# Token mixing and attention in one TensorE queue: the second half of the token mixing counted at twice its cost

## The chip, the cores and the metric

The kernel runs on one core of one Trainium2 chip. The metric is the time of one execution on the device, in microseconds (us), the median of several runs. Everything is float32.

A core has five engines that run beside each other, each with its own queue of instructions, worked off in the order in which the program issued them: TensorE (PE, matrix products, with a separate row PEld for loading weights), VectorE (DVE), ScalarE (ACT), GpSimd (POOL), and SyncE (SP), which here only starts DMA transfers. TensorE writes its products into PSUM, from where VectorE or ScalarE has to take them before the same buffer can be written again.

## The reference

Attention with normalised queries and keys for 8 batches, 12 heads, 448 positions and 64 columns, followed by an MLP mixer on the result:

```python
q_n, k_n = rmsnorm(q, g_q), rmsnorm(k, g_k)
scores = q_n @ k_n^T / sqrt(64)
attn = exp(scores - max);  attn = attn / (sum(attn) + 1e-9)
x = (attn @ v), heads side by side          # (8, 448, 768)

h  = relu(x^T @ w_tok1) @ w_tok2            # token mixing, inner size 256
u  = x + h^T
h2 = relu(u @ w_ch1) @ w_ch2                # channel mixing, inner size 1536
out = u + h2
```

## The kernel before

The kernel works batch by batch and always one batch ahead with the attention: while the mixer of batch b runs, the attention of batch b+1 is computed. The two are independent, and all of it goes through the same five queues. The program decides the order: it makes lists of work items, each a pair of an estimated cost (about microseconds) and a function that issues its instructions, and merges the lists:

```python
def merge(*lists):
    totals = [sum(c for c, _ in l) or 1.0 for l in lists]
    done = [0.0] * len(lists)
    at = [0] * len(lists)
    res = []
    while True:
        live = [i for i in range(len(lists)) if at[i] < len(lists[i])]
        if not live:
            return res
        i = min(live, key=lambda i: (done[i] + lists[i][at[i]][0] / 2) / totals[i])
        c, fn = lists[i][at[i]]
        at[i] += 1
        done[i] += c
        res.append((c, fn))
```

So the lists advance at the same share of their own totals. A cost has no other use but one: run() adds the costs up as a clock, by which a few DMA transfers are issued some microseconds later than the work that prepares them:

```python
def run(items):
    for c, fn in items:
        fn()
        clock[0] += c
        while pending and pending[0][0] <= clock[0]:
            pending.pop(0)[1]()
```

The main loop, with cuts:

```python
for b in range(B):
    early, double = middle_items(b)      # tok2, moving sums, ch1 | ch2, two columns of weights
    if b == 0:
        ...                              # batch 0 has a path of its own
    else:
        if in_next(b - 1):
            y, z = sends(b - 1, [0, 1, KC, KC + 1]), left
            left = [y[0], y[1], z[0], y[2], z[1], y[3]]
        run(merge(tok1_items(b, 0), left[:2]))
        begin, early = merge(tok1_items(b, 1) + early[:3 * KC], left[2:]), early[3 * KC:]
        if b == 1:
            early, double = merge(begin + early, sums[12:33]), merge(double, sums[33:])
            begin = []
        early = begin + early + double
    lo = (b + AHEAD) * per + 1
    att = []
    if b + AHEAD < B:
        att = att_items(lo, lo + 10) + x_items(b + AHEAD, 0) + att_items(lo + 10, lo + per)
    tail = 4
    early, last = early[:-tail], early[-tail:]
    if b + 1 < B:
        last = merge(last, x_items(b + 1, 1))
    run(merge(att, early) + last + last_items(b, sums[6:12]))
    left = turns(b, [2, KC + 2])
```

The items of the mixer, with their costs (us(n, cols) is n * cols * 4 / 2400):

- tok1, cost 2.56: four products of 384 columns (L638), then a ReLU on ScalarE. The first half of the token mixing is tok1 of the first 384 channels, and nothing of the attention lies beside it. The second half, begin, starts with tok1 of the other 384.
- tok2, cost 1.49, six of them: two products of 448 columns (L646), then VectorE adds the sum to uT (L651).
- moving_sums, cost 0, after every second tok2: two operations of VectorE, two of GpSimd (L667 to L670).
- ch1, cost 2.24, 21 of them (L770), and ch2, cost 2.24, 14 and 7 of them (L827). Each takes weights, a "unit" of 384 KB, from HBM; up to six units are held. A scheme with 7 products in place of 8 makes the operands by sums (L775, L836, L800). The four last of the 14 and the 7 single ones have no attention beside them: the tail of a batch.
- In left: four items that turn or send the last result of the batch before (L863, L582), cost 0.3. In batch 1 also sum items, which prepare sums of the weights.

The products of tok1, tok2, ch1 and ch2 all write into PSUM buffers called m_ps, of which there are two:

```python
ps_S = pool("ps_S", 4, space=PSUM)    # s_ps, d_ps: scores, sums of a row
ps_O = pool("ps_O", 2, space=PSUM)    # o_ps: attention times values
ps_M = pool("ps_M", 2, space=PSUM)    # m_ps
```

The attention of a batch is three groups t of two pairs of heads each, and a group is four steps s of about this form (cut):

```python
# for TensorE, one item "tiled" of cost 2.4 or 3.2
for k in ((0,), (1, 2), (3, 4), (5, 6))[s]: score(t, k)      # L338, then exp on ScalarE, L342
for k in ((), (0,), (1, 2), (3, 4))[s]:     values(pair, k)  # L412; k = 5, 6 in the next s = 0
# around it, for the other engines
s == 0: denominators of the group before (L441 to L458), loads of v and of the next keys/queries
s >= 1: group_sums es (GpSimd for k < 3, VectorE from there, L380)
s == 0, 1: squares (ScalarE, L1108), their sums (VectorE, L1122), s == 1: roots (12 small operations)
s == 2: scale (VectorE, L303), turn_qk of one pair (VectorE L318, ScalarE L321)
s == 3: turn_qk of the second pair, loads of the queries and keys after those (L1089)
```

The scores of a group need qkT from turn_qk of both of its pairs. Each step has several items, with costs between 0 and 0.6 for those that are not for TensorE.

Of the kernel before, what the change touches and what calls it, by code (L numbers as in the profile page):

```python
# [26 lines left out]
# [15 lines that stand above are left out]
# [3 lines left out]
def whole(ctx, tc, shifted, pre, q, k, v, g_q, g_k, moe_w_tok1, moe_w_tok2, moe_w_ch1, moe_w_ch2, out):  # L45
# [78 lines left out]
# [6 lines that stand above are left out]
# [135 lines left out]
    def weight_items(lo, hi):  # L265

        def one(i):
            if 3 <= i and i + 2 < len(chunks):
                weight_load(i + 2)
            convert_bits(i - 2)  # L270
            if i < len(chunks):
                convert_first(i)
            if 0 <= i - 1 < len(chunks):
                convert_second(i - 1)
            if 0 <= i - 2 < len(chunks):
                convert_last(i - 2)
            if 0 <= i - 3 - len(first):
                store(i - 3 - len(first))
        return [(1.0, lambda i=i: one(i)) for i in range(lo, hi)]
# [352 lines left out]
    def tok1(b, jc, h):  # L632
        cs = slice(h * HC, (h + 1) * HC)
        if h == 0:
            st["h1", jc] = h1_pool.tile([P, C], F32, name="h1")
        ps = m_tile()
        for c in range(NS):
            nc.tensor.matmul(  # L638
                out=ps[:, 0:HC], lhsT=w1_sb[0:R, c, jc * P:(jc + 1) * P], rhs=st["x", b, h][0:R, :, c, :],
                start=(c == 0), stop=(c == NS - 1))  # L640
        nc.scalar.activation(out=st["h1", jc][:, cs], in_=ps[:, 0:HC], func=AF.Relu)
# [223 lines left out]
    def turns(b, cs, send=True):  # L865

        def one(cc):
            trans_y(b, cc)
            if send:
                later(2.0, lambda: send_y(b, cc, st.pop(("y", cc))))  # L870
        return [(0.3, lambda cc=cc: one(cc)) for cc in cs]

    def sends(b, cs):
        return [(0.3, lambda cc=cc: send_y(b, cc, st.pop(("y", cc)))) for cc in cs]
# [3 lines left out]
    def x_items(b, h):  # L878
        return [(0.1, lambda j=j: trans_x(b, j)) for j in range(h * NC // 2, (h + 1) * NC // 2)]

    def tok1_items(b, h):
        return [(us(NS, HC), lambda j=j, h=h: tok1(b, j, h)) for j in range(NJ)]

    def middle_items(b):

        items = []
        for t in range(KC):
            items += [(us(NJ, S), lambda cc=cc: tok2(b, cc)) for cc in (t, KC + t)]
            if b:
                items.append((0.0, lambda t=t: moving_sums(b, t)))  # L890
        if b == 0:
            items += [(us(6, S), lambda mp=mp, o=o, j=j: ch1_first(mp, o, j))
                      for mp in range(KF // 2) for o in range(2) for j in range(2)]
            return items, [(us(6, S), lambda o=o, h=h, m=m: ch2_first(o, h, m))
                           for o in range(2) for h in range(2) for m in range(2)]
        items += [(us(6, HS), lambda mp=mp, i=i: ch1(b, mp, i)) for mp in range(KF // 2) for i in range(7)]
        return items, [(us(6, HS), lambda i=i, j=j: ch2(b, 0, i, j)) for i in range(7) for j in range(2)]

    def in_next(b):


        return b < B - 1 and not shifted

    def last_items(b, sums):

        single = [(us(6, HS), lambda i=i: ch2(b, 1, i, 0)) for i in range(7)]
        if b == 0:
            single = merge(
                [(us(6, S), lambda o=o, h=h: ch2_first(o, h, 2)) for o in range(2) for h in range(2)], sums)
        l = turns(b, [0, 1, KC, KC + 1], not in_next(b))  # L910
        return [single[0]] + merge(single[1:-1], l) + [single[-1]]
# [53 lines left out]
    for b in range(B):  # L965
        early, double = middle_items(b)
        if b == 0:
            begin = x_items(0, 1) + tok1_items(0, 0) + tok1_items(0, 1)
            early = merge(begin + early, weight_items(BEFORE, then)) + merge(
                double, weight_items(then, len(chunks) + 3) + sums[:6])  # L970
# [4 lines that stand above are left out]
                left = [y[0], y[1], z[0], y[2], z[1], y[3]]  # L975
            run(merge(tok1_items(b, 0), left[:2]))
            begin, early = merge(tok1_items(b, 1) + early[:3 * KC], left[2:]), early[3 * KC:]
            if b == 1:
                early, double = merge(begin + early, sums[12:33]), merge(double, sums[33:])
                begin = []  # L980
# [11 lines that stand above are left out]
# [182 lines left out]
def kernel(  # L1174
# [30 lines left out]
    with tc.If(nc.values_load(small[0:1, 0:1], min_val=0, max_val=1,  # L1205
                              skip_runtime_bounds_check_because="a comparison's result") > 0) as arm:
        whole(tc, False, pre, *args)
    with arm.Else():
        whole(tc, True, pre, *args)
# [30 lines left out]
```

## Time and profile before

| | |
|---|---|
| time, median of 3 runs | 1357.39 us (1355.1 to 1358.39) |
| span of the profiled execution | 1357.2 us |
| VectorE, ScalarE, GpSimd busy | 753.8, 365.1, 368.6 us |
| DMA, first queue | 494914 packets, 235.61 MB, 69.9% of 16 engines' span |
| HBM read, written | 197.85 MB, 39.52 MB |
| batch 1 | 278.4 to 446.1 us |
| batches 2, 3, 4, 5 | from 446.1, 603.9, 762.9, 921.0 us |
| batches 6, 7 | from 1079.3, 1232.1 us, to 1357.2 |

A batch is counted here from its first tok1. A line of the profile names the source line, the engine, the operation, the tile it writes and the tiles it reads; x16 says that 16 instructions were put together. A float32 product is two instructions. Square brackets hold how long the engine was idle before, and what ended that. "unit<-ws" is a transfer of weights into a unit.

### The profile page before, as it was taken

The numbers are of one execution on the slowest core, as the hardware profiler recorded it, in microseconds if no ns is written. First come the engines' busy times: TensorE is split into PE (matmuls) and PEld (weight loads), VectorE is DVE, ScalarE is ACT, GpSimd is POOL, SyncE is SP. The second block draws the span as 40 slices with busy tenths as digits, with TensorE's granted clock in tenths as the row PEclk, the third lists the DMA queues.
The fourth block names the chain that finished last, engine by engine and source line by source line (L and its number), as shares of the span: only waits on it lengthen the run. The fifth ranks groups of instructions, "written<-read, shape, count | busy, mean of one in ns | idle before, by whom it ended". The sixth has DMA issues, their size and how long they took to land.

```text
span 1357.2 us, 20152 instructions
## 1 busy us (share of the span) xinstructions
PE 1290.7 (95%) x7408; PEld 927.4 (68%) x7408; DVE 753.8 (56%) x1295; ACT 365.1 (27%) x734; POOL 368.6 (27%) x406
## 2 busy tenths in 40 slices
PE   4889998999998999999999999999999999999996
PEld 2444444446777577795778757795777867787996
DVE  6988897345763455635655265644556365543212
ACT  5554432023230233203331223302332023300100
POOL 1202211257662232302331123312323034211220
PEclk9899998999998999999999999999999999999998
DMA  9685778889989566594559765594665956476655
GB/s 197 185 246 171 223 190 224 231 206 233 267 228 239 113 169 157 129 249 103 135 143 198 173 147 124 135 247 98 167 157 132 240 116 160 123 179 139 181 172 113
DMA packets 508143, 238.83 MB, mean 176 GB/s; under 512 B 374084, under 2 KB 466628, under 8 KB 508036
## 3 DMA queue, kind: packets, MB, share of 16 engines
q1 hardware_dynamic: 494914, 235.61, 69.9%
q10 hardware_dynamic: 12994, 1.84, 0.8%
q8 instruction: 61, 1.00, 0.3%
q14 instruction: 46, 0.38, 0.1%
q0 software_dynamic: 128, 0.00, 0.0%
HBM read 197.85 MB, written 39.52 MB: 175 GB/s over the span
## 4 chain that ended last, share of the span: by engine, by line
PE 75%; DVE 11%; DMA 4%; ACT 2%; SPq 2%; issue 2%; POOL 1%; ACTq 1%; DVEq 0%
PE m_ps L827 21%; PE m_ps L770 19%; PE s_ps L338 8%; PE o_ps L412 7%; PE m_ps L638 6%; PE m_ps L751 4%; PE m_ps L733 4%; DMA unit<-ws 3%; PE m_ps L646 3%; DVE es L380 2%; DVE qk_t L303 2%; ACT e L342 1%; PE d_ps L392 1%; SPq L1089 1%; DVE qkT L318 1%
## 5 line engine op out<-in xcount | busy, mean ns | idle before, releaser
L827 PE MATMUL m_ps<-hb,unit 128*128 128x224 f32 x1764 | 343.5, 356 | 7.0 <-DMA unit<-ws 6.9
L827 PEld LDWEIGHTS m_ps<-hb,unit 128*128 128x128 f32 x1764 | 332.8, 191 | 24.1 <-issue 17.0
L770 PE MATMUL m_ps<-tu,unit 128*128 128x224 f32 x1008 | 202.8, 356 | 3.5 <-DVE r L775 3.0
L770 PEld LDWEIGHTS m_ps<-tu,unit 128*128 128x128 f32 x1008 | 188.3, 190 | 22.5 <-DVE r L775 5.5
L342 ACT ACTIVATE e<-s_ps 128x448 f32<-128x448 f32 x336 | 156.8, 546 | 95.4 <-PE s_ps L338 94.8
L770 PE MATMUL m_ps<-uT,unit 128*128 128x224 f32 x756 | 155.0, 357 | 6.6 <-ACT r L791 3.1
L770 PEld LDWEIGHTS m_ps<-uT,unit 128*128 128x128 f32 x756 | 140.4, 190 | 23.5 <-DVE uT L651 7.0
L338 PE MATMUL s_ps<-qkT 64*64 64x448 f32 x1260 | 148.6, 550 | 1.8 <-ACT x L618 1.6
L412 PE MATMUL o_ps<-e,v 64*64 64x448 f32 x1316 | 149.0, 540 | 0.1
L836 POOL TENSOR_TENSOR uT<-uT,r 128x448 f32<-128x448 f32 (+1 forms) x56 | 51.8, 936 | 268.2 <-DVE r L836 148.1
L775 DVE TENSOR_TENSOR r<-m_ps,r 128x448 f32<-128x448 f32 x63 | 38.9, 618 | 123.9 <-PE m_ps L770 82.1
L836 DVE TENSOR_TENSOR uT<-uT,m_ps 128x448 f32<-128x448 f32 (+1 forms) x70 | 34.0, 502 | 129.1 <-PE m_ps L827 129.1
L380 DVE TENSOR_TENSOR es<-es,e 128x896 f32<-128x896 f32 x84 | 93.9, 1118 | 14.6 <-ACT e L342 11.5
L412 PEld LDWEIGHTS o_ps<-e,v 64*64 64x64 f32 x1316 | 49.7, 133 | 68.2 <-issue 62.8
L338 PEld LDWEIGHTS s_ps<-qkT 64*64 64x64 f32 x1260 | 44.3, 133 | 73.6 <-issue 59.5
L775 POOL TENSOR_TENSOR hb<-r,r 128x448 f32<-128x448 f32 x21 | 27.9, 1327 | 227.0 <-ACT r L791 173.9
L380 POOL TENSOR_TENSOR es<-e 128x896 f32<-128x896 f32 x21 | 44.5, 2117 | 160.8 <-ACT e L342 160.8
L638 PE MATMUL m_ps<-x,w_sb 112*128 112x384 f32 x256 | 86.6, 492 | 0.0
L646 PE MATMUL m_ps<-w_sb,h 128*128 128x448 f32 x192 | 78.2, 550 | 6.6 <-DVE uT L651 6.6
L321 ACT ACTIVATE qkT<-qkT,g_t 128x448 f32<-128x448 f32 x36 | 24.0, 668 | 219.0 <-DVE qkT L318 219.0
L1122 DVE TENSOR_REDUCE ms<-sq 128x28 f32<-128x896 f32 (+2 forms) x47 | 51.2, 1090 | 45.1 <-ACT sq L1108 42.4
L638 PEld LDWEIGHTS m_ps<-x,w_sb 112*128 112x128 f32 x256 | 48.3, 192 | 36.0 <-ACT e L342 4.9
(100 smaller groups left out, 1352.8 us busy)
## 6 DMA issues: line engine op xcount, KB each, us to landing
unit<-ws SPq DMA_DIRECT2D x318, 384.0 KB, 4.1
raw<-in_moe_w_ch_dram SPq DMA_DIRECT2D x72, 256.0 KB, 3.7
v<-in_v_dram SPq DMA_DIRECT2D x94, 112.0 KB, 3.7
xs<-xt SPq DMA_DIRECT2D x56, 168.0 KB, 4.5
x<-xs SPq DMA_DIRECT2D x14, 672.0 KB, 6.9
out_dram<-turned SPq DMA_DIRECT2D x168, 56.0 KB, 2.1
ws<-stage SPq DMA_DIRECT2D x36, 256.0 KB, 3.9
raw<-ws SPq DMA_DIRECT2D x36, 256.0 KB, 4.9
```

The costliest lines, as they stand in the source:

```text
L338: nc.tensor.matmul(out=pss[i][rows_of(i, a), 0:S], lhsT=qkT[h, 1, k * D:(k + 1) * D], rhs=qkT[h, 0, :], start=True, stop=True)
L342: nc.scalar.activation(out=e[:, i, :], in_=pss[i][:, 0:S], func=AF.Exp)
L380: eng.tensor_tensor(out=es[:], in0=(es if k > 1 else st["e", t, 0])[:], in1=st["e", t, k][:], op=ALU.add)
L412: nc.tensor.matmul(out=st["o", p][a * D:(a + 1) * D, 0:S], lhsT=vt[rows, k * D:(k + 1) * D], rhs=e[rows, :], **kw)
L638: nc.tensor.matmul(out=ps[:, 0:HC], lhsT=w1_sb[0:R, c, jc * P:(jc + 1) * P], rhs=st["x", b, h][0:R, :, c, :], start=(c == 0), stop=(c == N ...
L646: nc.tensor.matmul(out=ps[:, 0:S], lhsT=st["h1", jc][:, cc * P:(cc + 1) * P], rhs=w2_sb[:, jc].rearrange("p c r -> p (c r)"), start=(jc == ...
L733: nc.tensor.matmul(out=ps[:, 0:S], lhsT=st["w"][t // KC][:, t % KC, j, :], rhs=u[:, t, :], start=(t == 0), stop=(t == 2 * KC - 1))
L751: nc.tensor.matmul(out=ps[:, 0:S], lhsT=w, rhs=natural(half)[:, :, t, :], start=(half == 0 and t == 0), stop=(half == 1 and t == KF - 1))
L770: nc.tensor.matmul(out=ps[:, j * HS:(j + 1) * HS], lhsT=w[:, t, j, :], rhs=m, start=(t == 0), stop=(t == KC - 1))
L775: add = lambda e, o, x, y: e.tensor_tensor(out=o, in0=x, in1=y, op=ALU.add)
L827: nc.tensor.matmul(out=ps[:, j * HS:(j + 1) * HS], lhsT=st["w"](j, t), rhs=hb[:, HB[what], t, :], start=(t == 0), stop=(t == KF - 1))
L836: add = lambda e, o, x, y: e.tensor_tensor(out=o, in0=x, in1=y, op=ALU.add)
```

## The change

```diff
             run(merge(tok1_items(b, 0), left[:2]))
             begin, early = merge(tok1_items(b, 1) + early[:3 * KC], left[2:]), early[3 * KC:]
+
+            begin = [(2 * c, fn) for c, fn in begin]
             if b == 1:
                 early, double = merge(begin + early, sums[12:33]), merge(double, sums[33:])
                 begin = []
```

Each item of the second half of the token mixing enters the merge with twice its cost, in all batches but the first. No instruction is added, removed or altered; what changes is the order in which the items of the mixer, of the attention and (in batch 1) the sums of weights are issued, and the clock of run(), which goes on twice as fast over these items. In the words that came with it, the change is to have beside the second half of the token mixing only half as much of the attention. Its purpose is to set the density of the attention's work there apart from that in the rest of the batch.

## The prediction

> **What bounds the kernel now.** I read the page's busy times first, then TensorE's waits, then the order of TensorE's work in one batch, then the chain of waits over the same stretch, and last a table of windows. The times are 1355.1, 1357.39 and 1358.39 us, so the kernel repeats within 0.3%.
>
> ```profile
> PE 1290.7 (95%) x7408; PEld 927.4 (68%) x7408; DVE 753.8 (56%) x1295; ACT 365.1 (27%) x734; POOL 368.6 (27%) x406
> ```
>
> TensorE (PE) is busy 95% of 1357.2 us, so all its idle time is 66.5 us. The waits say whose fault that is:
>
> ```profile
> PE t_ps L315 <- DVE g_t L945: 15.1, 1, 15.1
> PE s_ps L338 <- ACT e L342: 9.0, 3, 5.1
> PE m_ps L827 <- DMA unit<-ws: 6.9, 4, 5.2
> PE m_ps L646 <- DVE uT L651: 6.6, 6, 1.7
> PE m_ps L770 <- DVE r L775: 4.3, 9, 0.8
> PE m_ps L770 <- ACT r L791: 3.1, 5, 0.6
> ```
>
> The columns are the total, the number of waits and the longest, in us. The first is the start of the program; the change cannot touch it. What a change of order inside a batch can win is the rest: in batches 2 to 5 the second half of token mixing (L638, then L646) waits for VectorE's additions L651, and the first channel layer (L770) waits for L775 and L791. This is TensorE's work over that half in batch 2:
>
> ```profile
> 451.39 1.73 PE L338 MATMUL s_ps<-qkT 64*64 64x448 f32 x16
> 452.94 0.93 PE L412 MATMUL o_ps<-e,v 64*64 64x448 f32 x8
> 453.80 5.43 PE L638 MATMUL m_ps<-x,w_sb 112*128 112x384 f32 x16
> 459.06 1.67 PE L646 MATMUL m_ps<-w_sb,h 128*128 128x448 f32 x4
> ...
> 463.83 4.78 PE L646 MATMUL m_ps<-w_sb,h 128*128 128x448 f32 x12
> 468.54 1.74 PE L338 MATMUL s_ps<-qkT 64*64 64x448 f32 x16
> 470.09 1.68 PE L412 MATMUL o_ps<-e,v 64*64 64x448 f32 x16
> 472.74 3.36 PE L646 MATMUL m_ps<-w_sb,h 128*128 128x448 f32 x8 [0.96 <-DVE uT L651]
> 475.93 2.53 PE L770 MATMUL m_ps<-uT,unit 128*128 128x224 f32 x12
> 478.80 2.54 PE L770 MATMUL m_ps<-uT,unit 128*128 128x224 f32 x12 [0.34 <-DVE uT L651]
> ```
>
> Start, length, work. Three attention blocks lie beside this half (at 451.39, 460.66 and 468.54), and TensorE stands 0.96 + 0.34 = 1.3 us. The same two gaps come in batches 3, 4 and 5. Later in the batch there are 0.62, 0.17 and 0.76 us: the batch is 157.8 us long and TensorE idle for 2.9 us of it. The chain of waits names what the gaps hang on:
>
> ```profile
> 469.01 1.14 DVE es L380
> 470.15 2.00 DVE qk_t L303 x2
> 472.15 0.53 DVE uT L651
> 472.68 1.08 DVE qkT L318 x2
> 473.76 0.51 DVE uT L651
> ```
>
> VectorE (DVE) works without a break from 466 to 478.8, mostly for the attention (es L380, the scaling L303, the transposes L318), and the addition that would free the m_ps buffer stands in its queue behind them. Finally the windows:
>
> ```profile
> core 0: us, PE busy (x) PEld busy (x) DVE busy (x) ACT busy (x) POOL busy (x), PEclk, DMA share, GB/s
> 446.10:478.80 32.70, 31.40 (x158) 15.41 (x157) 17.98 (x34) 10.15 (x23) 7.67 (x6) 1.00 0.50 97
> 571.80:603.70 31.90, 31.90 (x172) 31.88 (x169) 14.08 (x27) 1.71 (x3) 4.81 (x6) 1.00 1.05 256
> ```
>
> Token mixing leaves the DMA engines half idle (0.50, 97 GB/s). The attention-free end of the batch has them full (1.05, 256 GB/s), though TensorE does not stand there in batch 2.
>
> **What the Trainium skill says.** "Perfetto Trace Analysis", section "Identifying Performance Opportunities", holds that the share of time in weight loads tells more about TensorE than its busy time, and that gaps repeating at the same place can mean too few buffers. Here the busy time is usable all the same: 36 matmuls of L770 take 7.01 us in the chain, 195 ns each, against a mean weight load of 190 ns, so they are issued as fast as weights load. The 0.96 and 0.34 us gaps do repeat in four batches, and m_ps has two buffers: it agrees. "TensorE: Matmul & The Clock Gate", section "Part 3: Packing small matmuls", says that small tiles run side by side in the array: 16 of L338 take 1.66 us, 104 ns each against 550 ns for one, so it agrees. Its "Part 1" says that an idle TensorE loses clock: after a wait of 5.22 us for a unit at 412 to 417.8 us, the window 416 to 433 has a granted clock of 0.83.
>
> **The change part by part.** No instruction is added or removed. One factor of 2 goes into the costs with which begin (tok1 of the second half, the six tok2, the moving sums, and four turns or sends of the last result) enters the merge. The rule takes the list whose finished share of its own total is smaller. begin costs 2 x 2.56 + 6 x 1.493 + 4 x 0.3 = 15.28; all of early before its last four items costs 84.72; the attention list of a batch 96.9. Before, begin is 15.28 / 84.72 = 18.0% of early, so 17.5 of the attention's 96.9 lies beside it. After, it is 30.56 / 100.0 = 30.6%, so 29.6 lies beside it. The change is described as putting only half as much attention there; by this rule **it puts 1.7 times as much there**, and I predict what the code does.
>
> Followed item by item for batch 2, the order after is: block s1, tok1, block s2, tok1, tok2, block s3, three tok2, block s0 of the next pairs, two tok2, then ch1. Four blocks instead of three lie beside begin, and they start earlier. The fourth, with its row sums, held TensorE from 481.3 to 485.0 in the trace: 3.7 us that only move. So TensorE's sum is unchanged, and only the gaps count.
>
> Gaps in begin after the change, with TensorE again starting at 451.4. Durations: blocks 2.4 and 3.2 us, tok1 2.7, tok2 1.5; on VectorE es 1.1, scaling 1.0, transpose 0.53, L651 0.53, moving sums 0.85, the 12 small operations for the roots 2.7.
> 1. TensorE reaches block s3 at 463.9 and would start the third tok2 at 468.6. VectorE has the roots until 463.4 (with one turn of the last result among them), then two es, two scalings and two transposes, and so adds tok2 number one at 468.7 to 469.2. Wait 0.65 us.
> 2. TensorE reaches the scores of the next pairs at about 474.3. They need qkT of the second pair. VectorE does two es (until 472.6), moving sums, a turn, an addition and two transposes (475.6), and ScalarE 0.67 us of scaling: 476.3. Wait 2.0 us.
> 3. The denominators (3.7 us of VectorE) now stand between the last two tok2 additions, so the last is added at about 483.95. TensorE wants that buffer at 482.9 for ch1. Wait 1.05 us.
> The sum is 3.7 us against 1.3 before, or +2.4 us.
>
> Back from this: ch1 and ch2 have 69% of the attention beside them instead of 82%. The 0.62 us wait at 492.7 came from denominators in VectorE's queue between 488.1 and 492.1; they have been moved away. Of the other 0.93 us I take a half as saved. So -1.1 us, and the net of batches 2 to 5 is +1.3 us each. For the attention-free tail, one item of 2.24 us longer with DMA engines already full, I add 0.2 us: **+1.5 us x 4 = +6**. Batch 6 has a shorter attention list (70.9) and no such gaps before (152.41 of 152.8 us busy); it gets 70.9 x 0.306 = 21.7 beside begin, more than the 17.5 that cost batch 2 1.3 us: **+1**. Batches 0 and 7 have nothing to gain: batch 0 is not touched, batch 7 has no attention beside it.
>
> Batch 1 stands apart: 167.7 us with TensorE idle for 9.7 us, of which 5.22 and 1.10 are waits for units in its tail. It alone has the 21 sum items merged in, and the DMA engines at 0.93 of the time. The factor moves the sums forward too (9 instead of 6 ahead of the second ch1 item) and lets attention loads leave earlier, when there is room. I take half of the 6.3 us and a little clock as won, against the same +2.4 us in begin: **-2 us**.
>
> Sum: +6 + 1 - 2 = +5 us, less 2 for the chance that waits of VectorE overlap more than in my hand order: **1360 us**.
>
> **The rivals.**
> (a) The attention's earlier loads pay: with more of it in the idle-DMA stretch the tails run free of DMA waits. For it: 0.50 against 1.05 in the windows, and 5.22 us in batch 1. Against it: all waits for units together are 10.9 us. It would make 1349 us.
> (b) VectorE becomes the bound of begin. For it: it is already unbroken for 13 us there, and the attention of a batch costs VectorE more (12 es, 6 scalings, 12 transposes, 6 reductions, the roots and 6 denominators at the durations above, about 52 us) than TensorE (about 380 small matmuls at 104 ns, 39 us). Against it: over begin its sum, some 23 us, stays under TensorE's 27. If the queries and keys of the next pairs also come late, because SyncE's queue stands until the last result is turned (10.9 us before), VectorE and ScalarE stall in order and each batch loses 4 us more: 1375 us.
> (c) Nothing: every gap moves, the sum stays. 1357 us.
>
> **Range and chances.** The terms are between -1 and +4 us for five batches and between -8 and +4 us for batch 1. Taken together: **1349 to 1373 us** for 8 in 10. Faster by over 2% means under 1330 us, which needs 27 us, more than the 22 us that TensorE is idle in batches 1 to 6 together, so 1%. Slower by over 2% means over 1384.5 us, which needs 5 us a batch: 4%. Within 2%: 95%.
>
> **What would show it.** Right: four blocks beside begin; in batches 2 to 5 waits for L651 of about 1 and 0.6 us and one of about 2 us of the scores for qkT (L321 or L318); no wait of 0.62 us for L791; a TensorE busy time within 5 us of 1290.7. The order of blocks would be wrong if three or fewer lay beside begin. Rival (a) would show as batches shorter than 157.8 us and a batch 1 under 162; rival (b) as VectorE waiting for sq (L1108) behind query and key loads, and batches over 161 us. Waits for units of over 1 us in the tails of batches 2 to 5 would show that I have the tail wrong.

## The result, and the profile after

| | before | changed |
|---|---|---|
| time, median of 6 runs each | 1356.1 us (1354.07 to 1358.39) | 1365.71 us (1364.79 to 1367.14) |
| ratio, with its 95% interval | | 1.0071 (1.0058 to 1.0084) |
| span of the profiled execution | 1357.2 us | 1364.3 us |
| batch 1 | 167.8 us, TensorE idle 9.7 | 166.8 us, idle 7.7 |
| batches 2, 3, 4, 5 | 157.6, 159.0, 158.1, 158.3 us | 159.7, 160.2, 159.7, 160.1 us |
| TensorE idle in each of them | 2.85, 3.44, 2.85, 2.86 us | 4.78, 5.15, 4.80, 4.80 us |
| batch 6 | 152.8 us, idle 0.4 | 154.8 us, idle 1.4 |

The kernel became 0.7% slower. The idle time of a batch is the sum of the gaps that the timeline of TensorE shows in it. The four batches 2 to 5 together are 6.7 us longer, batch 6 is 2.0 us longer, batch 1 is 1.1 us shorter, and the start with batches 0 and 7 makes up -0.6 us: together 7.0 us, the difference of the two spans before rounding. (Batch 2 is 157.6 us here and not 157.8: batch 3 of the kernel before begins at 603.7 us, batch 6 at 1079.1 and batch 7 at 1231.9.)

The page of the changed kernel has TensorE as busy as before, within half a microsecond:

```profile
PE 1291.2 (95%) x7408; PEld 925.3 (68%) x7408; DVE 745.8 (55%) x1295; ACT 365.4 (27%) x734; POOL 359.3 (26%) x406
```

So nothing was made dearer (VectorE's and GpSimd's sums are even 8.0 and 9.3 us smaller); the loss is idle time of TensorE. The waits of TensorE in the changed kernel:

```profile
PE m_ps L770 <- DVE hb L775: 7.3, 4, 1.8
PE m_ps L770 <- ACT r L779: 6.4, 9, 0.8
PE m_ps L646 <- DVE uT L651: 6.0, 7, 2.3
PE s_ps L338 <- ACT qkT L321: 5.2, 4, 1.3
PE m_ps L827 <- DMA unit<-ws: 4.8, 4, 2.6
```

Two of these are new in size: 7.3 us in four waits for L775, and 5.2 us in four waits of the scores for qkT. Four is the number of the batches 2 to 5. The timeline of TensorE in batch 2 shows where they lie:

```profile
449.93 1.74 PE L338 MATMUL s_ps<-qkT 64*64 64x448 f32 x16
...
455.13 1.73 PE L338 MATMUL s_ps<-qkT 64*64 64x448 f32 x16
...
462.58 1.73 PE L338 MATMUL s_ps<-qkT 64*64 64x448 f32 x16
...
467.73 3.27 PE L646 MATMUL m_ps<-w_sb,h 128*128 128x448 f32 x8 [0.22 <-DVE uT L651]
470.94 1.73 PE L412 MATMUL o_ps<-e,v 64*64 64x448 f32 x16
472.49 0.92 PE L338 MATMUL s_ps<-qkT 64*64 64x448 f32 x4
474.71 0.59 PE L338 MATMUL s_ps<-qkT 64*64 64x448 f32 x2 [1.30 <-ACT qkT L321]
...
476.36 3.27 PE L646 MATMUL m_ps<-w_sb,h 128*128 128x448 f32 x8
479.47 2.43 PE L770 MATMUL m_ps<-uT,unit 128*128 128x224 f32 x12
482.52 2.62 PE L770 MATMUL m_ps<-uT,unit 128*128 128x224 f32 x12 [0.62 <-ACT r L779]
...
511.18 7.08 PE L770 MATMUL m_ps<-tu,unit 128*128 128x224 f32 x36 [0.81 <-ACT r L779]
...
530.27 2.54 PE L770 MATMUL m_ps<-uT,unit 128*128 128x224 f32 x12 [1.83 <-DVE hb L775]
```

Four blocks of attention now stand ahead of the first ch1 at 479.47, the fourth split by a wait: its first scores run from 472.49, the rest only from 474.71. The gaps are 0.22, 1.30, 0.62, 0.81 and 1.83 us, 4.78 in sum. In the kernel before, the gaps of batch 2 in ch1, behind the two in the token mixing, were these:

```profile
492.73 2.54 PE L770 MATMUL m_ps<-uT,unit 128*128 128x224 f32 x12 [0.62 <-ACT r L791]
522.94 2.54 PE L770 MATMUL m_ps<-uT,unit 128*128 128x224 f32 x12 [0.17 <-DVE r L775]
536.41 2.54 PE L770 MATMUL m_ps<-tu,unit 128*128 128x224 f32 x12 [0.76 <-DVE r L775]
```

The largest gap now is the 1.83 us. The chain of waits says what VectorE did ahead of it:

```profile
524.00 0.62 DVE r L775
524.63 0.57 DVE dt L441
...
525.46 0.51 DVE dt L441
...
526.24 0.51 DVE rd L455
...
526.78 0.62 DVE uT L458
527.40 0.56 DVE rd L455
...
527.99 0.62 DVE uT L458
528.61 1.07 DVE hb L800 x2
529.68 0.55 DVE hb L775
```

Between two additions (L775) that each free an m_ps buffer, the denominators of two pairs (L441 to L458) and then two sums (L800) go through VectorE: 5.1 us in which TensorE can run two products of about 2.3 us, and then it stands. In the windows the half of the token mixing (first line) and the attention-free tail (second) look as before, with DMA at 0.49 and 1.03:

```profile
core 0: us, PE busy (x) PEld busy (x) DVE busy (x) ACT busy (x) POOL busy (x), PEclk, DMA share, GB/s
444.70:477.00 32.30, 30.78 (x171) 13.37 (x170) 17.12 (x33) 11.49 (x25) 6.88 (x6) 1.00 0.49 89
570.20:604.30 34.10, 34.10 (x184) 34.08 (x181) 14.04 (x27) 1.71 (x3) 4.81 (x6) 1.00 1.03 263
```

### The profile page after: what moved, and what is told of

Read it like the earlier page. It is cut to its first block, busy times and chain, and to the rows that moved or that the text cites. A ratio compares the mean times of both kernels' runs of the same rounds, so it can differ in the third digit from the quotient of the medians.

```text
span 1364.3 us, 20138 instructions
## 1 busy us (share of the span) xinstructions
PE 1291.2 (95%) x7408; PEld 925.3 (68%) x7408; DVE 745.8 (55%) x1295; ACT 365.4 (27%) x734; POOL 359.3 (26%) x406
## 4 chain that ended last, share of the span: by engine, by line
PE 76%; DVE 12%; DMA 4%; ACT 3%; issue 2%; SPq 1%; POOL 1%; DVEq 0%; ACTq 0%; POOLq 0%
PE m_ps L827 23%; PE m_ps L770 22%; PE s_ps L338 7%; PE o_ps L412 6%; PE m_ps L638 4%; PE m_ps L751 4%; PE m_ps L733 4%; PE m_ps L646 2%; DMA unit<-ws 2%; DVE qk_t L303 2%; DVE qkT L318 1%; PE d_ps L392 1%; ACT e L342 1%; DVE ms L1124 1%; DVE es L380 1%
## 5 line engine op out<-in xcount | busy, mean ns | idle before, releaser
L770 PE MATMUL m_ps<-tu,unit 128*128 128x224 f32 x1008 | 200.6, 355 | 3.2 <-ACT r L779 3.2
L770 PEld LDWEIGHTS m_ps<-tu,unit 128*128 128x128 f32 x1008 | 189.1, 190 | 15.9 <-issue 7.1
L342 ACT ACTIVATE e<-s_ps 128x448 f32<-128x448 f32 x336 | 157.4, 546 | 115.7 <-PE s_ps L338 112.3
L770 PE MATMUL m_ps<-uT,unit 128*128 128x224 f32 x756 | 155.2, 357 | 11.4 <-DVE hb L775 7.3
L770 PEld LDWEIGHTS m_ps<-uT,unit 128*128 128x128 f32 x756 | 140.3, 190 | 31.7 <-DVE hb L775 8.7
L775 DVE TENSOR_TENSOR r<-m_ps,r 128x448 f32<-128x448 f32 x63 | 39.2, 622 | 138.0 <-PE m_ps L770 116.1
L1124 DVE TENSOR_REDUCE ms<-sq 128x28 f32<-128x896 f32 (+2 forms) x47 | 51.3, 1091 | 71.6 <-ACT sq L1110 67.7
L646 PE MATMUL m_ps<-w_sb,h 128*128 128x448 f32 x192 | 82.1, 569 | 6.0 <-DVE uT L651 6.0
L646 PEld LDWEIGHTS m_ps<-w_sb,h 128*128 128x128 f32 x192 | 35.4, 194 | 49.2 <-issue 33.1
```

What stands on the lines that cost most here:

```text
L342: nc.scalar.activation(out=e[:, i, :], in_=pss[i][:, 0:S], func=AF.Exp)
L646: nc.tensor.matmul(out=ps[:, 0:S], lhsT=st["h1", jc][:, cc * P:(cc + 1) * P], rhs=w2_sb[:, jc].rearrange("p c r -> p (c r)"), start=(jc == ...
L770: nc.tensor.matmul(out=ps[:, j * HS:(j + 1) * HS], lhsT=w[:, t, j, :], rhs=m, start=(t == 0), stop=(t == KC - 1))
L1124: self.nc.vector.tensor_reduce(out=st["ms", p][:, p % 2, lo:hi], in_=sq[:, lo:hi], axis=AX_X, op=ALU.add)
```

## The experiments

My theory: TensorE loses where a run of VectorE's work for the attention stands in its queue ahead of something TensorE waits for; what counts is which pieces come to stand next to each other. The rivals: the density of the attention beside the token mixing counts, whatever stands where; or transfers and SyncE's queue (the clock of run(), the sends of the last result) make the loss.

| run | ratio to before (95%) | batches 2 to 5, us |
|---|---|---|
| factor 0.5 | 1.0050 (1.0037 to 1.0064) | 157.5, 156.6, 158.4, 158.5 |
| factor 2, old clock | 1.0068 (1.0049 to 1.0088) | 159.7, 160.3, 159.7, 159.8 |
| no denominators, changed | 0.9965 (0.9956 to 0.9975) | 156.7, 156.7, 156.7, 156.7 |
| no denominators, before | 0.9936 (0.9913 to 0.9958) | 156.7, 156.1, 155.7, 156.4 |
| half of es, changed | 0.9904 (0.9877 to 0.9930) | 157.4, 157.5, 157.4, 157.4 |
| half of es, before | 0.9889 (0.9855 to 0.9924) | 155.6, 155.6, 155.6, 155.6 |
| denominators spread, before | 0.9979 (0.9968 to 0.9989) | 158.1, 155.9, 156.2, 157.2 |
| denominators spread, changed | 1.0205 (1.0187 to 1.0222) | 163.3, 163.3, 163.3, 161.6 |
| k = 3 on GpSimd, before | 0.9961 (0.9948 to 0.9974) | 156.5, 156.9, 157.2, 157.0 |
| spread, GpSimd, factor 2 in batch 1 | 1.0051 (1.0033 to 1.0069) | 160.2, 159.0, 157.3, 160.3 |
| k = 3 on GpSimd, changed | 1.0049 (1.0033 to 1.0065) | 159.9, 159.4, 159.1, 159.9 |
| GpSimd, factor 2 in batch 1 | 0.9960 (0.9945 to 0.9975) | 157.0, 158.1, 156.7, 158.2 |

### Half as much, as the words have it

```diff
-            begin = [(2 * c, fn) for c, fn in begin]
+            begin = [(0.5 * c, fn) for c, fn in begin]
```

> The factor is 0.5 in place of 2, so that by the merge rule only 9.6 of the attention's 96.9 lies beside the second half of the token mixing (17.5 in the kernel before, 29.6 in the changed one): two blocks in place of three, none of them between the second and the fourth tok2. Theory 1 (TensorE waits where VectorE's work for the attention stands ahead of an m_ps addition): no wait for L651 or for qkT in that half, 1.3 us less than before there; in ch1 and ch2 the attention is denser (90% of it in place of 82%), so waits there of 1.5 to 3 us a batch; in sum 1352 to 1360 us. Theory 2 (the density beside the token mixing alone sets the loss): monotonic, so about 4 us faster than before, 1352 us. Theory 3 (transfers gain or lose by the order): the attention's loads crowd into the stretch with the fuller DMA engines, waits for units in the tails, over 1362 us.

Measured: 1364.1 us, ratio 1.0050. The order came as worked out: in the token mixing of batches 2 to 5 no wait is left, and these batches have 1.7 to 3.1 us of idle time against 2.85 to 3.44 before. But the whole is slower, and most of that is in batch 1: 173.8 us in place of 167.8, with 14.8 us idle. Two lines of TensorE's waits in this kernel:

```profile
PE m_ps L827 <- DMA unit<-ws: 11.9, 10, 6.5
...
PE m_ps L770 <- DVE hb L775: 2.9, 1, 2.9
```

The 2.9 us are in batch 1, where the chain has two scalings, two transposes, two es and two sums of VectorE (with exponentials of ScalarE between them) ahead of that addition. The longest wait for a unit, 6.5 us, is in batch 1 too, and the other nine are spread over the tails of batches 1 to 5. Of the 5.1 us by which TensorE's idle time in batch 1 grew, 1.7 us are waits in the second half of the token mixing, 1.8 us waits in ch1, and 1.6 us waits for units. Batch 6 is 2.5 us longer as well.

So the time is not monotonic in the factor: 0.5, 1 and 2 give 1.0050, 1 and 1.0071. Batches 2 to 5 alone are: they take 631.0, 633.0 and 639.7 us, and their waits in that half are 0, 1.3 and 2.1 us each, so in them density is not refuted by this run. What speaks against it is batch 1: with one block of the attention ahead of the fifth tok2 in place of three, TensorE waited there for L651 longer than before, 1.50 and 1.86 us against 1.11 and 0.41; VectorE had a sum of squares (L1124) and the roots of the attention between these additions. Theory 1 was right about the token mixing of batches 2 to 5 and said nothing of batch 1, so its 1352 to 1360 us was a miss; the theory of transfers had a share here.

### The factor 2 without the faster clock

```diff
+            cost = {id(fn): c for c, fn in begin}
             begin = [(2 * c, fn) for c, fn in begin]
...
-        run(merge(att, early) + last + last_items(b, sums[6:12]))
+        items = [(cost.get(id(fn), c), fn) for c, fn in merge(att, early) + last]
+        run(items + last_items(b, sums[6:12]))
```

(The second part for all batches but the first.)

> As the changed kernel, with the factor 2 in the merge, but the clock of run() advances by the old costs, so only the order of items counts and no transfer is put off less than before. Theory 1 (order on VectorE's queue): same time as the changed kernel, 1364 to 1367 us, with the waits of 1.30, 0.62, 0.81 and 1.83 us in every batch from 2 to 5. Rival (the faster clock sends the last result too early, and SyncE's queue, which stands until it has been turned, holds up the loads of queries and keys): most of the loss of about 9 us goes, under 1360 us.

Measured: 1366.22 us, 1.0068, with 1.30, 0.62, 0.81 and 1.83 us in each of the batches 2 to 5, to the hundredth. So the clock of run() has no visible part in the loss; the order of the items is what is left.

### Without the denominators

```diff
 def begin(p):
     ps = st.pop(("d", p))
+    if p >= NPAIR:
+        return
 ...
 def end(p):
+    if p >= NPAIR:
+        nc.vector.tensor_copy(out=uT of the pair, in_=o_ps of the pair)
+        return
```

The results of these two kernels are not divided by the row sums.

> The changed kernel without the denominators of all batches but the first: the two transposes, the reciprocal and the third transpose of each pair are left out and the values are only copied out of PSUM, so the result is not divided by the row sums. Per pair of heads some 2.0 us less on VectorE. Theory 1: the wait of 1.83 us (additions L775 behind the denominators of the third group) goes, and with it the one of 0.62 us; those of 1.30 and 0.81 us, which hang on es, the scaling and qkT, stay. The changed kernel loses 2 to 2.5 us a batch, 10 to 14 us in all, so about 1352 to 1356 us. Rival (the loss is not VectorE's but that of TensorE's order or of transfers): time within 3 us of the changed kernel, 1363 us or more.

> The kernel before with the same left out. Theory 1: the waits of 0.62 us (492.7) and 0.76 us go, the two of 0.96 and 0.34 us stay; 1.0 to 1.4 us a batch, 5 to 8 us in all, so 1348 to 1351 us, and the gap between changed and before shrinks from 9.6 us to 3 to 6 us. Rival: the gap stays at 9 to 10 us whatever the denominators cost.

Measured: 1352.42 us (0.9965) for the changed kernel and 1348.8 us (0.9936) for the one before. TensorE's timeline of the changed kernel without denominators, around the place of the 1.83 us:

```profile
510.11 7.08 PE L775 MATMUL m_ps<-tu,unit 128*128 128x224 f32 x36 [0.81 <-ACT r L784]
...
522.66 2.43 PE L775 MATMUL m_ps<-tu,unit 128*128 128x224 f32 x12
524.93 4.70 PE L775 MATMUL m_ps<-uT,unit 128*128 128x224 f32 x24
529.47 2.43 PE L775 MATMUL m_ps<-tu,unit 128*128 128x224 f32 x12
```

(L775 and L784 are the L770 and L779 of the other kernels here.) The 24 products from 524.93 on run without a break where 1.83 us lay. The 0.62 us is gone in all four batches too; 1.30 and 0.81 us stay, as expected. In the kernel before the 0.62 and 0.76 us go. So the denominators hold 2.45 us of the 4.8 us of idle time in a changed batch and 1.38 of the 2.9 before. The gap between the two kernels shrinks from 1.0071 to 0.9965 / 0.9936 = 1.0029.

### With half of the row sums on VectorE

```diff
+        n = 2 if k < 3 else 1
-        eng.tensor_tensor(out=es[:], in0=(es if k > 1 else ...)[:], in1=st["e", t, k][:], op=ALU.add)
+        eng.tensor_tensor(out=es[:, 0:n], in0=(es if k > 1 else ...)[:, 0:n], in1=st["e", t, k][:, 0:n], op=ALU.add)
```

These leave four of seven blocks of keys out of the row sums of every second pair.

> The changed kernel with half of the VectorE part of the row sums: from k = 3 on only the first pair of each group is added to es, so four additions of 1.1 us a group become about 0.55 us each, and the row sums of every second pair leave out four of seven blocks of keys. Some 6.6 us less on VectorE a batch. Theory 1: the wait of 1.30 us (two es stand ahead of the qkT transposes) shrinks to under 0.4 us and the one of 0.81 us, behind two es and two scalings, to under 0.3; the 1.83 us behind the denominators stays. 1 to 2 us a batch, 5 to 10 us in all: 1355 to 1361 us. Rival (not VectorE): within 2 us of the changed kernel.

> The kernel before with the same left out. Theory 1: the waits of 0.96 and 0.34 us in the second half of the token mixing go, since four es stand in VectorE's queue there, and the later ones stay in part: 1.3 to 1.8 us a batch, 1348 to 1351 us. The gap to the changed kernel with the same left out stays at 5 to 10 us, since in both the part that hangs on es is of the same size. Rival (not VectorE): within 2 us of the kernel before.

Measured: 1345.6 us and 1342.98 us (the kernel before took 1360.23 us beside them). In the changed batches 2 to 5 the 1.30 us became 0.41, the 0.81 and 0.22 us went, the 0.62 and 1.83 us stayed to the hundredth. In the kernel before the 0.96 and 0.34 us went and 0.62 and 0.76 stayed. Both sets of waits are as expected. The totals are not: they lie 9 and 5 us below my ranges. By the spans the changed kernel lost 21.7 us and the kernel before 18.4; batches 2 to 5 have 10.0 and 10.6 us of that, and batch 0, beside which es is added up too, is 6.4 and 3.9 us shorter, which I had not counted. Nor did the gap between the two stay at 5 to 10 us: the medians differ by 2.6 us. In batches 2 to 5 there is still 1.8 us between them in each (157.4 against 155.6), but batches 0 and 1 are now shorter in the changed kernel, by 1.8 and 2.2 us.

### The denominators spread, nothing left out

```diff
-            items += part(denominators((p - 2, p - 1)))
+            items += part(denominators((p - 2, p - 1)), 1.4 if t > NPAIR else 0.4)
```

> The kernel before, with a cost of 1.4 instead of 0.4 for each of the four parts of the denominators (from batch 1 on), so that the merge puts them one or two to a ch1 item instead of four behind one; nothing is left out. Theory 1: no four of them stand in a row ahead of an addition L775, so the waits of 0.62 and 0.76 us go. The attention list becomes longer by 12, so 19.6 in place of 17.5 lies beside the second half of the token mixing, and the waits for L651 there may change by half a us either way. 0.5 to 1.5 us a batch less, 1350 to 1355 us. Rival (the length of VectorE's work between two additions is not what counts, only its sum): same time as before within 1 us.

> The changed kernel with the same cost of 1.4. Theory 1: the wait of 1.83 us for L775 becomes under 0.5 us and that of 0.62 us goes or shrinks; the one for qkT (1.30 us) comes earlier, as the list puts 33 of 108.9 beside the second half of the token mixing, and may grow to 2 us. In sum 1 to 2 us a batch less than the changed kernel, 1357 to 1361 us. Rival (density alone): even more of the attention beside that half, so slower than the changed kernel, over 1366 us.

Measured: 1356.3 us, 0.9979, on the kernel before, and 1386.02 us, 1.0205, on the changed one. On the kernel before the 0.62 and 0.76 us went, but the 0.34 us for L651 became 1.32, and waits for units of 2.25, 0.32 and 1.18 us came up in the tails of three batches, so the time is just above the 1350 to 1355 us that I expected. This run settles more of the rival of density: in batch 2 three blocks stand beside the second half of the token mixing as before, the second and the third one tok2 earlier, and VectorE has the same instructions; yet the waits there are 2.2 us (0.88 and 1.32) in place of 1.3, no less than the 2.1 us with four blocks in the changed kernel.

On the changed kernel the 1.83 us became 0.87, and the wait for qkT grew from 1.30 to 3.64 us, past what I expected; I had a gain. The time is what the rival of density alone had called for, over 1366 us. These are VectorE's lines in the changed kernel:

```profile
468.77 2.32 DVE L380 TENSOR_TENSOR es<-es,e 128x896 f32<-128x896 f32 x2 [0.56 <-ACT e L342]
...
472.80 1.15 DVE L318 STREAM_TRANSPOSE qkT<-qk_t 128x448 f32<-128x448 f32 x2
```

and these with the denominators spread, with TensorE's wait as the last:

```profile
471.27 2.29 DVE L380 TENSOR_TENSOR es<-es,e 128x896 f32<-128x896 f32 x2 [1.09 <-ACT e L342]
473.48 0.61 DVE L651 TENSOR_TENSOR uT<-uT,m_ps 128x448 f32<-128x448 f32 x1
474.01 0.39 DVE L667 TENSOR_TENSOR tu<-uT 128x224 f32<-128x224 f32 x1
474.43 0.73 DVE L668 TENSOR_TENSOR tu<-uT,tu 128x224 f32<-128x224 f32 x1
475.08 0.63 DVE L863 STREAM_TRANSPOSE turned<-uT 128x448 f32<-128x448 f32 x1
475.64 0.60 DVE L318 STREAM_TRANSPOSE qkT<-qk_t 128x448 f32<-128x448 f32 x1
476.17 0.57 DVE L651 TENSOR_TENSOR uT<-uT,m_ps 128x448 f32<-128x448 f32 x1
476.68 0.62 DVE L318 STREAM_TRANSPOSE qkT<-qk_t 128x448 f32<-128x448 f32 x1
...
478.05 0.94 PE L338 MATMUL s_ps<-qkT 64*64 64x448 f32 x2 [3.64 <-ACT qkT L321]
```

The two es start 24.09 us after the batch's first tok1 in both kernels (the batch begins at 444.68 and 447.18 us). But TensorE comes to these scores 1.50 us earlier in its batch, since three tok2 and not four stand ahead of them, and VectorE is done with the transposes 0.84 us later, since two additions L651 and not one stand among them and L668 takes 0.73 us in place of 0.39. The two make up the 2.34 us by which the wait grew. The rival with SyncE's queue is not the cause: the chain of waits names a transfer ahead of the turn of the last result (L863), but that landed at 474.55 us, while VectorE was still at L668, and VectorE has no gap from 471.27 us to the end of the transposes.

### One addition to GpSimd

```diff
-        eng = nc.gpsimd if k < 3 else nc.vector
+        eng = nc.gpsimd if k < 3 + (t >= 9) else nc.vector
```

> The kernel before, but from the attention of batch 3 on the addition to es of k = 3 goes to GpSimd (2.1 us there) in place of VectorE (1.1 us): three instructions a batch. Theory 1: 1.1 us less in VectorE's queue ahead of L651, so the waits of 0.96 and 0.34 us in batches 2 to 5 fall to under 0.5 in sum; the others stay, unless the addition of k = 4 now waits for GpSimd and holds VectorE's queue up. 0.5 to 1 us a batch less, 1352 to 1356 us. Rival (GpSimd and VectorE slow each other, or VectorE stands for k = 3): 1357 to 1362 us.

> The changed kernel with the addition to es of k = 3 on GpSimd from the attention of batch 3 on, nothing left out. If the wait for qkT (1.30 us) and that of 0.81 us hang on the two es in VectorE's queue ahead of the transposes, one es less takes about 1.1 us off the first and about 0.8 off the second: 1.5 to 2 us a batch, 6 to 8 us in all, so 1358 to 1361 us beside 1357 to 1359 for the kernel before; the 1.83 us behind the denominators stays. Rival (SyncE's queue, which stands until the last result is turned, sets the time of qkT): the wait of 1.30 us stays, 1364 us or more.

Measured: 1353.62 us, 0.9961, on the kernel before; 1363.48 us, 1.0049, on the changed one. On the first the 0.96 us went and 0.34 stayed, as expected. On the second the 0.81 us went, and the 1.30 us stayed, which I had given to the rival. SyncE is not its cause, though. This is what VectorE did there (e11):

```profile
458.69 0.65 DVE L863 STREAM_TRANSPOSE turned<-uT 128x448 f32<-128x448 f32 x1
459.26 1.54 DVE L1165 SCALAR_TENSOR_TENSOR nt<-rs 128x56 f32<-128x56 f32 x1
...
467.74 2.32 DVE L380 TENSOR_TENSOR es<-es,e 128x896 f32<-128x896 f32 x2 [0.56 <-ACT e L342]
```

and this GpSimd:

```profile
458.64 2.08 POOL L380 TENSOR_TENSOR es<-es,e 128x896 f32<-128x896 f32 x1 [3.61 <-ACT e L342]
```

The small operation L1165, 0.22 us otherwise, took 1.54 us and ended with the moved addition: the 1.1 us taken off VectorE came back as 1.3. In the kernel before, the same addition ran at 461.56 to 463.64, where VectorE was idle. And the two es that follow wait for the exponentials of the third block (0.56 us), which stand behind qkT of the first pair on ScalarE. The wait for qkT thus hangs on a chain through VectorE and ScalarE: transposes of the first pair, ScalarE's scaling, exponentials, two es, the transposes of the second pair. Whether the two es that I had named, k = 3 and 4, stand in that chain, this run cannot say, since what it took off came back. With half of es, which shortened them and k = 5 and 6, the first pair's transposes start 0.93 us sooner after TensorE's third block of scores and the second pair's 1.37 us sooner.

### All together, and two of the three

> All that helped by the theory: factor 2 in batch 1 alone (1.1 us less there in the profile of the changed kernel), 1.4 for the denominators, k = 3 on GpSimd from batch 3 on. If the parts add up: 1348 to 1353 us, the fastest of all; at least 155.5 us a batch stay, since TensorE's own work is about 155 us. Rival (each moves the others' blocks, so that the waits only change places): 1355 us or more.

```diff
+            if b == 1:
+                begin = [(2 * c, fn) for c, fn in begin]
```

with both edits above. Measured: 1366.59 us, 1.0051: the rival was right. In batches 2 to 5 the waits in ch1 are all gone, but 1.4 us for L651 and 1.8 to 3.5 us for units in the tails have come up, and batch 1 took 173.7 us.

> The kernel before with k = 3 on GpSimd (which by itself took 0.4% off) and the factor 2 in batch 1 alone, where the changed kernel's batch was 1.1 us shorter. If the two add up: 1 us less than with GpSimd alone, a ratio to the kernel before of 0.995 to 0.997, which the runs may not tell from the 0.9961 of GpSimd alone; batch 1 takes 166.5 to 167 us. Rival (batch 1's gain was a chance of its tail's transfers): batch 1 takes 168 us or more.

The same without the spread denominators. Measured: 1351.8 us, 0.9960 (0.9945 to 0.9975). Batch 1 took 166.5 us, as expected; the whole cannot be told from GpSimd alone (0.9961). Both beat the kernel before and the changed one.

## Why the prediction was right, and where it was wrong

The time, 1365.71 us, lies in the range of 1349 to 1373, within 2%; the figure of 1360 was too low, 2.6 us above the kernel before where 9.6 us were measured. By the steps:

- **The direction of the change.** Right: the factor puts more of the attention beside the second half of the token mixing, four blocks and not three. With the factor 0.5 there are two.
- **TensorE's sum stays.** Right: 1290.7 and 1291.2 us busy. Everything is in the gaps.
- **The three gaps in that half.** Right in place, too large in size: 0.65, 2.0 and 1.05 us were predicted, 0.22, 1.30 and 0.62 measured, 2.1 in place of 3.7. The third ended with ScalarE's copy L779 and not with the last L651, but it goes with the denominators, as the run without them showed.
- **The 1.1 us back in ch1.** This step failed. The prediction said of the denominators that "they have been moved away", and took half of the rest as saved, because ch1 has less attention beside it. In fact the gaps in ch1 rose from 1.55 to 2.64 us (0.81 + 1.83). The 0.62 us at 492.7 did go, but the denominators of the next group came to stand ahead of the sums L800, and made 1.83 us. Thinner attention did not mean fewer gaps; the run without denominators shows that this gap is theirs: it went with them, in all four batches.
- **Batches 2 to 5 together.** +6 us predicted, +6.7 us measured. The two errors above (1.6 us too much a batch in the token mixing, 2.2 us too little in ch1) nearly cancelled. That the sum came out is luck.
- **The tail.** +0.2 us a batch for full DMA engines: not seen. There are no waits for units in the tails of batches 2 to 5 of the changed kernel.
- **Batch 6.** +1 us predicted, +2.0 measured (waits of 0.41 and 0.95 us for L651, and the rest not in gaps).
- **Batch 1.** -2 predicted, -1.1 measured: waits for units fell from 6.3 to 4.8 us, the waits in the second half of the token mixing, with one of 0.62 us at the second ch1, rose from 1.7 to 2.9 us, and the 1.7 us in the rest of ch1 went. The working of the prediction does not give its own -2: half of 6.3 us against 2.4 leaves -0.75, and the other 1.25 us were put down to the clock without a reckoning.
- **The 2 us taken off for overlap** had the wrong sign: the spans differ by 7.0 us, the medians by 9.6.

Of the rivals, (a), loads that pay, has only the 1.1 us of batch 1. (b), VectorE as the bound with queries and keys late, did not come: ScalarE's wait for the loads of queries and keys in batch 2 is 4.6 us, against 5.1 before. With the spread denominators batches 2 to 5 do go over 161 us, but by the order in VectorE's queue: ScalarE's wait for these loads is 4.6 us there too. (c) is out by the interval.

The difference of the medians is larger than that of the spans because of the executions that were profiled: the one of the kernel before took 1359.03 us, 2.9 above its median, that of the changed kernel 1366.05 us, 0.3 above.

What stays open: the part of batch 6's 2.0 us that is not in gaps, about 1 us, and whether a third m_ps buffer would have hidden the waits. No run tried one.

## What to carry to other kernels

Where one engine is busy for 95% of the time and others feed it in order, read which pieces stand next to each other in the feeders' queues, and not only how dense the work is on average: here a cost that shifted one list against another moved every later meeting of the two, and waits turned up in places that the edit does not touch. Two such shifts do not add, as the run with all three edits showed. The safest gain here was to take work out of the feeder's queue without moving anything else, and that only where the engine that took it over did not hold up the feeder (0.9961 on the kernel before; on the changed one the 1.30 us stayed).

## What the runs showed of the hardware

- GpSimd and VectorE can hold each other up. In the changed kernel with k = 3 on GpSimd, an operation of VectorE with two operands in SBUF and 56 columns (L1165) took 1.54 us in place of 0.22 beside an addition on GpSimd, and ended within 0.1 us of it, while a transpose with one operand (L863, 0.65 us) ran beside the same addition at its usual length. The Trainium skill, "SBUF — State Buffer", section "SBUF: two separate sides", says that the two share a pair of ports, that an operation of VectorE with two SBUF inputs needs it against a GpSimd operation that reads SBUF, and that whichever comes second waits for the whole instruction. The trace agrees.
- After a wait of 3.64 us (474.4 to 478.05 in the changed kernel with spread denominators) TensorE's granted clock was below full for some microseconds in batches 2 to 4, which added to the wait. The windows of batch 2:

```profile
447.20:475.00 27.80, 26.99 (x153) 11.68 (x151) 13.59 (x26) 9.85 (x22) 4.90 (x3) 1.00 0.42 81
475.00:480.00 5.00, 1.95 (x10) 0.73 (x12) 2.30 (x5) 1.32 (x3) 0.66 (x1) 0.82 0.48 76
480.00:486.00 6.00, 6.00 (x16) 2.38 (x12) 2.74 (x7) 0.32 (x1) 1.29 (x2) 0.87 0.69 119
486.00:500.00 14.00, 12.85 (x81) 10.00 (x84) 7.88 (x14) 5.47 (x12) 5.61 (x5) 1.00 0.57 163
```

The column before the last two is the clock: 1.00, 0.82, 0.87, 1.00. Batches 2 to 4 of that run are 163.3 us long. Batch 5 has the same gaps, but its clock stayed at 1.00 after the wait, and it is 161.6 us long; why it was spared is not shown. After the wait of 1.83 us in the changed kernel the clock is 1.00.
